# Attention outputs stored unnormalized with their row sums, and divided where the experts gather them

## Chip, cores and metric

One Trainium2 chip, one of its cores. The metric is the device time of one execution in microseconds (us). The engines are named as in the profile: PE (matmul) and PEld (its weight loads), DVE (vector), ACT (scalar), POOL (GpSimd) and SP, which only issues DMAs.

## The reference

Thresholded attention over 8 batches and 8 heads with 576 positions of 64 numbers each, followed by a mixture of 8 experts to which a hash of the token's id assigns each of the 4608 tokens.

```python
def _attn_ref(q, k, v, tau) -> np.ndarray:
    scale = 1.0 / np.sqrt(q.shape[-1])
    scores = scale * np.matmul(q, k.transpose(0, 1, 3, 2))
    thresh = np.max(scores, axis=-1, keepdims=True) - tau
    scores = np.where(scores >= thresh, scores, -1000000000.0)
    scores = scores - np.max(scores, axis=-1, keepdims=True)
    attn = np.exp(scores)
    attn = attn / (np.sum(attn, axis=-1, keepdims=True) + 1e-09)
    return np.matmul(attn, v).astype(np.float32)
...
    x = np.ascontiguousarray(attn_out.transpose(0, 2, 1, 3)).reshape(B * S, H * D)
...
    expert_idx = token_ids * np.int64(2654435761) % np.int64(E)
    for e in range(E):
        mask = expert_idx == e
        xe = x[mask]
        h = np.maximum(xe @ w1[e], 0.0)
        out[mask] = h @ w2[e]
```

x has 4608 rows of 512 numbers; w1 is 8 x 512 x 1024, w2 is 8 x 1024 x 512. All is float32.

## The kernel before

**Order.** The kernel is written with the Tile layer, inside blocks of `manual_schedule`: within such a block each engine runs its instructions in the order in which they stand in the program. The attention with all that runs beside it is one block, and the last steps of expert 0's first layer and the loop over the experts are others. An engine starts an instruction when its semaphores allow, and nothing behind it on that engine starts sooner.

**Attention.** Two heads of one batch make a pair p; there are 32 pairs, NP, in the order hp (which two heads, 0 to 3), then batch. A pair has five steps s; step n of the whole loop is 5p + s. Step 0 holds the last 64 rows of both heads, steps 1 to 4 hold 128 rows of each. A step's work is spread over three steps of the loop:

- `score` (L222, PE): scores into one of two PSUM buffers `sc`.
- `negate` (L233, DVE): copies -score into `ns` with the row's minimum, which frees `sc`; POOL makes the threshold `thr` (L240).
- `expo` (L247, ACT): exp into `w`.
- `mask` (L258, DVE), one step later: drops what is under the threshold, and gives the row sums `rs`.
- `turn_w` (L269, PE), two steps later: turns w through the single PSUM buffer `tr`; `put_wT` (L285 and L290, ACT) copies it to SBUF.
- `av_part` (L300, PE): the product with v into the PSUM tile `av`, a pair later, at steps 1 to 4; `put_oT` (L316, ACT) copies its halves.
- `turn_o` (L269, PE), two pairs later at step 0: turns them back into `av`, rows on partitions.
- `add_eps` (L330, POOL), L686 (DVE, reciprocal) and `put_xm` (L339, DVE): row sums plus 1e-9, their reciprocals, and the multiplication out of `av` into `xm`. Three DMAs on SP (L345, L350) then write xm to the DRAM tensor `x_scratch` of 4608 x 512, in pieces of 128 numbers.

The next `av_part` overwrites `av`, so it has to wait until `av` has been read.

**Routing** is done beside the attention, by small DVE instructions (`route`) and by POOL's DMAs (`scatters`).

**Expert 0 early.** From pair 26 on, POOL gathers for expert 0's five blocks kt of 128 rows the pieces hp = 0, 1, 2 (`fetch_early`, `fetch_0`, L113): 15 gathers, three for each block, at the steps 3, 4 and 0. At the last step (n = 160, LAST, and after) `early_xT` turns them, and `early_h` multiplies them with w1: 48 parts, called through `fill`, eight blocks of 128 columns, each into one of the two `sc` buffers, which a DVE copy (L594) frees. After the last pair's output come, in program order, the DVE copies of the indices (L753 to L761), the rest of `route` (to L488), the five gathers of the pieces hp = 3, `fill` for 30 parts, and `early_xT` for the last pieces (L563, L577). `late_h` adds the missing quarter.

**Experts.** For each expert two layers run, as products of seven blocks (`seven`, L859) with sums beforehand and afterwards on DVE (L791, L794) and copies on ACT; four PSUM buffers `bank2` rotate. `fetch(e)` gathers five blocks of whole rows of x into `xg`, `turn_x` turns them: five DVE transposes (L956) into `xq`, and 16 DMAs on SP (`move`, L964) into `xT`. Both are called from `side1` and `side2`, which run between the products of the two layers. `put_out` writes the results. A last loop takes rows beyond an expert's capacity, as many blocks as the routing counts.

## Time and profile before

| | us |
|---|---|
| median of 3 runs (949.88 to 950.99) | 950.64 |
| the profiled execution | 951.87 |
| its span, first to last instruction | 950.2 |
| PE busy in the span | 935.2 (98%) |
| DVE busy | 733.9 (77%) |
| ACT busy | 478.6 (50%) |
| POOL busy | 306.2 (32%) |
| L258, DVE, 288 instructions | 225.9 |
| L247, ACT, 288 instructions | 220.3 |
| L233, DVE, 288 instructions | 205.3 |

The attention takes about the first 455 us, expert 0's early part lies on its end, and from about 500 us on the experts run. The page has the span in 40 slices of 23.75 us, each digit a busy share in tenths. A row of a group gives the line, the engine, the operation, out<-in by the program's names with shapes, the count, and then busy time and mean time of one. A row in order of time begins with its start and its length in us; in brackets stands the idle time before it and what ended it. One engine's rows can overlap, since its instructions are pipelined. A matmul's end is modelled, its start is not.

### The profile page before, as it was taken

Reading aid. Unit: us, or ns where it says so; the run is one execution under the profiler, and the core shown is the slowest. Engines: PE = TensorE matmul, PEld = TensorE weight load, DVE = VectorE, ACT = ScalarE, POOL = GpSimd, SP = SyncE. Lnnn points to the kernel's source line nnn. Section 1 sums busy time; section 2 is a strip of 40 time slices with the busy share of each in tenths; the row PEclk is TensorE's granted clock in tenths of the full one; section 3 lists DMA queues with packets and bytes.
Section 4 is the critical chain, followed back from the end, with each engine's and each line's share of the span. In section 5 each row is a group of like instructions: output and inputs, shape, how many; then the busy total and the mean of one; then the engine's idle time right before and its main releaser. Section 6 shows DMA issues by size and latency. Waiting matters only on the chain. (4 is left out here: it accounts for less than half of the span.)

```text
span 950.2 us, 21041 instructions
## 1 busy us (share of the span) xinstructions
PE 935.2 (98%) x7779; PEld 645.2 (68%) x7779; DVE 733.9 (77%) x1638; ACT 478.6 (50%) x778; POOL 306.2 (32%) x413
## 2 busy tenths in 40 slices
PE   7999999999999999999999999999999999999996
PEld 4666666666666666666667777777777777777784
DVE  7999999999999999999456756756667566575541
ACT  6988888888898898888320211202112031120310
POOL 4233233237766733565043300403013030110202
PEclk9999999999999999999999999999999999999999
DMA  7355456445438857841017444344443445311101
GB/s 177 87 142 131 107 134 148 100 124 137 105 90 212 210 158 156 196 103 35 26 37 216 156 93 174 96 147 160 115 151 91 143 157 142 128 55 32 50 1 51
DMA packets 113510, 113.31 MB, mean 119 GB/s; under 512 B 31182, under 2 KB 88014, under 8 KB 113408
## 3 DMA queue, kind: packets, MB, share of 16 engines
q1 hardware_dynamic: 105168, 92.84, 36.9%
q0 software_dynamic: 7808, 18.91, 6.7%
q8 instruction: 63, 1.03, 0.5%
q14 instruction: 39, 0.32, 0.1%
q10 hardware_dynamic: 432, 0.21, 0.1%
HBM read 81.99 MB, written 21.72 MB: 109 GB/s over the span
## 5 line engine op out<-in xcount | busy, mean ns | idle before, releaser
L247 ACT ACTIVATE w<-ns,nmx 128x576 f32<-128x576 f32 x288 | 220.3, 776 | 32.8 <-DVE ns L233 32.5
L258 DVE SCALAR_TENSOR_TENSOR w<-ns,thr,w 128x576 f32<-128x576 f32 x288 | 225.9, 816 | 0.7 <-POOL thr L240 0.6
L233 DVE TENSOR_SCALAR_CACHE_REDUCE ns<-sc 128x576 f32<-128x576 f32 x288 | 205.3, 744 | 4.4 <-PE sc L222 3.5
L222 PE MATMUL sc<-k_sb,q 64*128 64x288 f32 (+1 forms) x1280 | 178.7, 423 | 1.1 <-DVE drop L650 0.6
L269 PEld LDWEIGHTS tr<-ident,w 64*128 64x128 f32 x2624 | 106.6, 139 | 88.4 <-ACT wT_b L290 26.4
L240 POOL TENSOR_SCALAR thr<-nmx,drop 128x2 f32<-128x2 f32 (+1 forms) x160 | 103.4, 646 | 184.0 <-DVE ns L233 173.3
L938 POOL DMA_INDIRECT out_dram<-o_sb,gidx x39 | 47.7, 1222 | 292.3 <-ACT o_sb L934 278.9
L269 PE MATMUL tr<-ident,w 64*128 64x64 f32 x2624 | 139.0, 230 | 2.6 <-ACT wT_a L290 2.0
L869 ACT COPY p<-bank 128x600 f32<-128x600 f32 (+1 forms) x22 | 14.4, 654 | 201.4 <-PE bank L859 200.6
L222 PEld LDWEIGHTS sc<-k_sb,q 64*128 64x128 f32 (+1 forms) x1280 | 92.5, 178 | 23.1 <-DVE ns L233 9.9
L300 PE MATMUL av<-wT_a,v 128*64 128x320 f32 (+1 forms) x704 | 100.7, 419 | 0.0
L859 PE MATMUL bank<-h,w_sb 128*128 128x300 f32 (+1 forms) x384 | 97.3, 410 | 0.9 <-DVE h L609 0.9
L866 ACT ACTIVATE h<-h 128x600 f32<-128x600 f32 x56 | 39.4, 703 | 114.6 <-DVE h L794 114.1
L290 ACT COPY wT_a<-tr 128x512 f32<-128x512 f32 (+1 forms) x128 | 81.7, 638 | 19.8 <-PE tr L269 19.5
L859 PE MATMUL bank<-xT,w_sb 128*128 128x300 f32 x336 | 89.4, 416 | 0.0
L859 PEld LDWEIGHTS bank<-h,w_sb 128*128 128x128 f32 x384 | 72.9, 190 | 22.9 <-DVE h L609 1.3
L290 ACT COPY wT_b<-tr 128x512 f32<-128x512 f32 (+1 forms) x128 | 81.2, 635 | 6.6 <-PE tr L269 4.3
L300 PE MATMUL av<-wT_b,v 128*64 128x256 f32 x640 | 83.2, 389 | 0.0
L859 PEld LDWEIGHTS bank<-xT,w_sb 128*128 128x128 f32 x336 | 63.9, 190 | 21.0
L859 PE MATMUL bank<-h_s,w_s 128*128 128x300 f32 (+1 forms) x256 | 64.3, 410 | 0.0
L300 PEld LDWEIGHTS av<-wT_a,v 128*64 128x64 f32 x704 | 43.9, 137 | 28.8 <-issue 0.3
L859 PE MATMUL bank<-x_s,w_s 128*128 128x300 f32 x224 | 61.5, 423 | 0.0
(147 smaller groups left out, 1110.3 us busy)
## 6 DMA issues: line engine op xcount, KB each, us to landing
w_sb<-in_moe_w_dram SPq DMA_DIRECT2D x16, 2048.0 KB
q<-in_q_dram SPq DMA_DIRECT2D x62, 288.0 KB
v<-in_v_dram SPq DMA_DIRECT2D x32, 256.0 KB
x_scratch<-xm SPq DMA_DIRECT2D x32, 256.0 KB
xT<-xq SPq DMA_DIRECT2D x84, 80.0 KB
k_sb<-in_k_dram SPq DMA_DIRECT2D x31, 144.0 KB
k_sb<-in_k_dram SPq DMA_DIRECT2D x32, 112.0 KB
x_scratch<-xg SPq DMA_DIRECT2D x9, 256.0 KB
```

What stands on the lines that cost most here:

```text
L222: nc.tensor.matmul(sc[out_rows, i, 0:S2], lhsT=q_sb[rows, h, q0:q1], rhs=k_sb[rows, h], start=True, stop=True)
L233: nc.vector.tensor_scalar(out=ns[:].rearrange("p (i s) -> p i s", i=2), in0=sc[:, :, 0:S2], scalar1=-1.0, scalar2=None, op0=ALU.mult, op1= ...
L240: nc.gpsimd.tensor_scalar(out=thr[:, 0:j + 1], in0=stats[n][0][:, 0:j + 1], scalar1=drop[:], scalar2=None, op0=ALU.add)
L247: nc.scalar.activation(w, nss[n, j][:], AF.Exp, bias=stats[n][0][:, j:j + 1], scale=-1.0)
L258: nc.vector.scalar_tensor_tensor(out=w, in0=nss.pop((n, j))[:], scalar=stats[n][1][:, j:j + 1], in1=w, op0=ALU.is_le, op1=ALU.mult, accum_ ...
L269: nc.tensor.transpose(dst[:, r, 64 * c:64 * c + 64], src[rows, c0:c0 + P], ident[rows, rows])
L290: nc.scalar.copy(dst, tr[:, :, 0:64 * n_c].rearrange("p r (c q) -> p r c q", c=n_c))
L300: nc.tensor.matmul(av[64 * j:64 * j + 64, g, c0:c1], lhsT=v_sb[:, c, 64 * j:64 * j + 64], rhs=wT[g][:, i, c0:c1], start=(c == 0), stop=stop)
L859: nc.tensor.matmul(ps[:, i, 0:width], lhsT=x[:, c, c0:c0 + P], rhs=y[:, c], start=c == 0, stop=c == n_k - 1)
L866: nc.scalar.activation(c, c, AF.Relu)
L869: nc.scalar.copy(p1, product(a11, b11))
L938: inst = nc.gpsimd.indirect_dma_start(out=out[:, :], out_offset=bass.IndirectOffsetOnAxis(ap=idx, axis=0), in_=o_sb, in_offset=None, bound ...
```

## The change

- `x_scratch` gets rows of 4 x 144 numbers instead of 4 x 128. A piece of 144 holds 8 numbers, 128 of data, and 8 numbers; the two heads' row sums stand in its columns 7 and 136. `xg` grows in the same way.
- `add_eps` writes the row sums plus 1e-9 into `xm` itself (two tiles that are kept, by turns). The reciprocal at step 2 is gone.
- `put_xm` is an ACT copy of `av` into `xm`, without a factor. At step 0 it stands ahead of `expo`; before, the DVE instruction stood behind `negate` and `expo`.
- A new `divide` on DVE takes the reciprocals of the sums in gathered rows and multiplies the rows by them. It is called for the early pieces of expert 0 at step 2 of pairs 27 to 31, for its last pieces behind their gathers, ahead of the transposes for each block of the other experts, and in the last loop.
- Turning x for expert e + 2 begins at the end of expert e's second layer (two blocks), and ends in the first half of the next expert's first layer; before, it lay in both halves of that first layer.

```diff
-    x_dram = nc.dram_tensor("x_scratch", (N, DIN), FP32, kind="Internal").ap()
+    XP = P + 16
+    XW = HP * XP
+    x_dram = nc.dram_tensor("x_scratch", (N, XW), FP32, kind="Internal").ap()
...
-        gather(x_rows, xg_bufs[kt][:, P * hp:P * hp + P], gidx_0[:, kt, hp:hp + 1])
+        gather(x_rows, xg_bufs[kt][:, XP * hp:XP * hp + XP], gidx_0[:, kt, hp:hp + 1])
+
+    def pieces_of(x, hp0, hp1):
+
+        return x[:, XP * hp0:XP * hp1].rearrange("p (h m) -> p h m", h=hp1 - hp0)
+
+    def x_sums(x, hp0=0, hp1=HP):
+        return pieces_of(x, hp0, hp1)[:, :, 7:2 * D + 9:2 * D + 1]
+
+    def x_data(x, hp0=0, hp1=HP):
+        return pieces_of(x, hp0, hp1)[:, :, 8:2 * D + 8]
+
+    def divide(x, hp0=0, hp1=HP):
+        rec = consts_r.tile([P, HP, 2], FP32, name="rec")[:, 0:hp1 - hp0]
+        nc.vector.reciprocal(rec, x_sums(x, hp0, hp1))
+        data = x_data(x, hp0, hp1).rearrange("p h (j d) -> p h j d", j=2)
+        nc.vector.tensor_tensor(out=data, in0=data,
+                                in1=rec[:, :, :, None].to_broadcast([P, hp1 - hp0, 2, D]),
+                                op=ALU.mult)
...
+            xm = xm_bufs[p % 2]
             rs = rss.pop(p)
-            for i, cols in ((0, 9), (9, 1)):
-                nc.gpsimd.tensor_scalar(out=rec[:, i:i + cols], in0=rs[:, i - i // 9:i - i // 9 + cols],
-                                        scalar1=1e-9, scalar2=None, op0=ALU.add)
-            recs[p] = rec
+            cols = slice(7, 2 * D + 9, 2 * D + 1)
+            for dst, src in ((xm[:, 0:NQ, cols], rs[:, 0:8].rearrange("p (t j) -> p t j", j=2)),
+                             (xm[:, NQ, cols], rs[:, 8:9].to_broadcast([P, 2]))):
+                nc.gpsimd.tensor_scalar(out=dst, in0=src, scalar1=1e-9, scalar2=None, op0=ALU.add)
...
-            nc.vector.tensor_tensor(
-                out=xm[:].rearrange("p t (j d) -> p t j d", j=2),
-                in0=av[:, :, 0:NS * D].rearrange("p j (t d) -> p t j d", t=NS),
-                in1=rec[:].rearrange("p (t j) -> p t j", j=2)[:, :, :, None]
-                .to_broadcast([P, NS, 2, D]), op=ALU.mult)
+            xm = xm_bufs[p % 2]
+            nc.scalar.copy(xm[:, :, 8:2 * D + 8].rearrange("p t (j d) -> p t j d", j=2),
+                           av[:, :, 0:NS * D].rearrange("p j (t d) -> p t j d", t=NS))
...
+        nc.vector.memset(x_sums(xg_bufs[0]), 1.0)
+        for xm in xm_bufs:
+            nc.vector.memset(xm[:, :, 0:8], 0.0)
+            nc.vector.memset(xm[:, :, 2 * D + 8:XP], 0.0)
...
-                if s == 2 and 0 <= q < NP:
-                    nc.vector.reciprocal(recs[q][:], recs[q][:])
+                if s == 2 and 0 <= n - G0 - 7 < NS * KT:
+                    divide(xg_bufs[(n - G0 - 7) // NS], 0, HP - 1)
...
                     negate(n, 0)
+                    if s == 0 and p >= 2:
+                        put_xm(p - 2)
                     expo(n, 0)
                 if s == 0 and p > 0 and not placed:
                     next(pieces)
-                if s == 0 and p >= 2 and n != LAST:
+                if n == LAST + NS:
                     put_xm(p - 2)
...
             for kt in range(KT):
                 fetch_0(kt, HP - 1)
+            for kt in range(KT):
+                divide(xg_bufs[kt], HP - 1, HP)
             fill(FO * 2 * (CO - 1) - 18)
...
-                return lambda: nc.vector.transpose(
-                    out=xq[:, :, 32 * k:32 * k + 32],
-                    in_=xg_bufs[k][:].rearrange("p (d a) -> p d a", a=32))
+                def both():
+                    divide(xg_bufs[k])
+                    nc.vector.transpose(
+                        out=xq[:, :, 32 * k:32 * k + 32].rearrange("p (h b) a -> p h b a", h=HP),
+                        in_=x_data(xg_bufs[k]).rearrange("p h (b a) -> p h b a", a=32))
+                return both
...
-                turns = turn_x(e + 1) if more else []
+                turns = pend if e else turn_x(1)
+                pend = []
...
-                        if step > 2:
-                            run(turns, 1 if g == 0 else 2)
+                        if g == 0 and step > 2:
+                            run(turns, 1 if step < 5 else 6)
...
                         if e + 2 < E:
                             fetch(e + 2)
+                            pend.extend(turn_x(e + 2))
                     else:
                         run(x_work, 2)
+                    if step == 5:
+                        run(pend, 2)
...
             gather(x_dram, xg_bufs[0][:], idx[:, 0:1])
+            divide(xg_bufs[0])
```

More of the change, by code (lines that the diff above doesn't have):

```diff
@@ L79 @@
     w_pool = ctx.enter_context(tc.tile_pool(name="w_pool", bufs=2))
+    consts_r = ctx.enter_context(tc.tile_pool(name="consts_r", bufs=2))
     sc_stack = ctx.enter_context(ExitStack())
@@ L104 @@
     ov_i = consts.tile([P, NOV + 1], I32, name="ov_i")
-    xg_bufs = [consts.tile([P, DIN], FP32, name=f"xg_{i}") for i in range(KT)]
+    xg_bufs = [consts.tile([P, XW], FP32, name=f"xg_{i}") for i in range(KT)]
     xT_0 = consts.tile([P, CO, CAP], FP32, name="xT_0")
@@ L135 @@
          tc.tile_pool(name="a_o", bufs=1) as a_o, \
-         tc.tile_pool(name="a_x", bufs=2) as a_x, \
+         tc.tile_pool(name="a_x", bufs=1) as a_x, \
          tc.tile_pool(name="rt_sb", bufs=1) as rt_sb, \
@@ L158 @@
         av = ps_av.tile([P, 2, 512], FP32, name="av")
-        kts, rss, recs, scs, nss, stats, ws = {}, {}, {}, {}, {}, {}, {}
+        xm_bufs = [a_x.tile([P, NS, XP], FP32, name=f"xm_{i}") for i in range(2)]
+        kts, rss, scs, nss, stats, ws = {}, {}, {}, {}, {}, {}
         def load_pair(p):
@@ L322, in x_place @@
             hp, b = divmod(p, B)
-            return b * S, hp * P
+            return b * S, hp * XP
         def add_eps(p):
-            rec = a_st.tile([P, 2 * NS], FP32, name="rec")
+            xm = xm_bufs[p % 2]
             rs = rss.pop(p)
-            for i, cols in ((0, 9), (9, 1)):
-                nc.gpsimd.tensor_scalar(out=rec[:, i:i + cols], in0=rs[:, i - i // 9:i - i // 9 + cols],
-                                        scalar1=1e-9, scalar2=None, op0=ALU.add)
-            recs[p] = rec
+            cols = slice(7, 2 * D + 9, 2 * D + 1)
+            for dst, src in ((xm[:, 0:NQ, cols], rs[:, 0:8].rearrange("p (t j) -> p t j", j=2)),
+                             (xm[:, NQ, cols], rs[:, 8:9].to_broadcast([P, 2]))):
+                nc.gpsimd.tensor_scalar(out=dst, in0=src, scalar1=1e-9, scalar2=None, op0=ALU.add)
         def put_xm(p):
-            rec = recs.pop(p)
-            xm = a_x.tile([P, NS, P], FP32, name="xm")
-            nc.vector.tensor_tensor(
-                out=xm[:].rearrange("p t (j d) -> p t j d", j=2),
-                in0=av[:, :, 0:NS * D].rearrange("p j (t d) -> p t j d", t=NS),
-                in1=rec[:].rearrange("p (t j) -> p t j", j=2)[:, :, :, None]
-                .to_broadcast([P, NS, 2, D]), op=ALU.mult)
+            xm = xm_bufs[p % 2]
+            nc.scalar.copy(xm[:, :, 8:2 * D + 8].rearrange("p t (j d) -> p t j d", j=2),
+                           av[:, :, 0:NS * D].rearrange("p j (t d) -> p t j d", t=NS))
             r0, c0 = x_place(p)
             nc.sync.dma_start(
-                out=x_dram[r0:r0 + TAIL, c0:c0 + P].rearrange("(t p) m -> p t m", p=P),
+                out=x_dram[r0:r0 + TAIL, c0:c0 + XP].rearrange("(t p) m -> p t m", p=P),
                 in_=xm[:, 0:NQ])
             for j in range(2):
-                cols = slice(D * j, D * j + D)
-                nc.sync.dma_start(out=x_dram[r0 + TAIL:r0 + S, c0 + D * j:c0 + D * j + D],
-                                  in_=xm[64 * j:64 * j + 64, NQ, cols])
+                cols = slice(XP // 2 * j, XP // 2 * j + XP // 2)
+                nc.sync.dma_start(
+                    out=x_dram[r0 + TAIL:r0 + S, c0 + XP // 2 * j:c0 + XP // 2 * j + XP // 2],
+                    in_=xm[64 * j:64 * j + 64, NQ, cols])
         def route():
@@ L563, in early_xT @@
                     nc.tensor.transpose(tr[:, r // 64, 64 * i:64 * i + r1 - r],
-                                        xg_bufs[kt][r:r1, P * co:P * co + P],
+                                        xg_bufs[kt][r:r1, XP * co + 8:XP * co + 8 + P],
                                         ident[r:r1, r:r1])
@@ L677 @@
                     nc.sync.dma_start(
-                        out=x_dram[r0:r0 + DIN, DIN - P:].rearrange("(t p) m -> p t m", p=P),
-                        in_=xg_bufs[0][:].rearrange("p (t m) -> p t m", m=P))
+                        out=x_dram[r0:r0 + DIN, XW - XP:].rearrange("(t p) m -> p t m", p=P),
+                        in_=xg_bufs[0][:].rearrange("p (t m) -> p t m", m=XP))
                 q = p - 1
@@ L1054 @@
             gather(x_dram, xg_bufs[0][:], idx[:, 0:1])
+            divide(xg_bufs[0])
             tr = bank2()
             for co in range(CO):
-                nc.tensor.transpose(tr[:, 0, co * P:co * P + P], xg_bufs[0][:, co * P:co * P + P],
-                                    ident[:])
+                nc.tensor.transpose(tr[:, 0, co * P:co * P + P],
+                                    xg_bufs[0][:, co * XP + 8:co * XP + 8 + P], ident[:])
             nc.vector.tensor_copy(xT_0[:, :, 0:P], tr[:, 0].rearrange("p (c q) -> p c q", c=CO))
```

## The prediction

> **What bounds the kernel now.** I read the page's slices first, then the windows, one per pair of heads, then the rows in order of time.

> ```profile
> PE   7999999999999999999999999999999999999996
> DVE  7999999999999999999456756756667566575541
> ```

> Up to slice 19 (about 452 us) two engines look full; afterwards only PE does. Of the two, one sets the pace and the other keeps up. The windows of two pairs (columns: length; busy PE, PEld, DVE, ACT, POOL with counts; clock, DMA share, GB/s):

> ```profile
> 298.89:312.78 13.89, 13.89 (x179) 8.81 (x176) 13.83 (x39) 12.29 (x21) 9.85 (x13) 1.00 0.49 110
> 312.78:326.67 13.89, 13.89 (x178) 8.81 (x175) 13.83 (x39) 12.28 (x21) 9.65 (x12) 1.00 0.97 257
> ```

> DVE is within 0.06 us of full, which invites the reading that 0.85 us taken off it shortens each pair. A matmul's end is modelled, so PE's busy time proves nothing; I compare starts. The PE rows below hold the same product of twelve and of eight matmuls twice: in the pair above, and in the last pair, where there are no scores left, ACT has little to do, and DVE sits idle for 7.15 and 5.10 us before its next row.

> ```profile
> 307.46 1.51 PE L300 MATMUL av<-wT_b,v 128*64 128x256 f32 x12
> 308.90 0.52 PE L269 MATMUL tr<-ident,w 64*128 64x64 f32 x10
> ...
> 310.66 1.08 PE L300 MATMUL av<-wT_b,v 128*64 128x256 f32 x8
> 311.68 0.52 PE L269 MATMUL tr<-ident,w 64*128 64x64 f32 x10
> ...
> 464.53 1.52 PE L300 MATMUL av<-wT_b,v 128*64 128x256 f32 x12
> 465.98 1.28 PE L587 MATMUL sc<-xT,w_sb 128*128 128x300 f32 x4
> 467.19 1.08 PE L300 MATMUL av<-wT_b,v 128*64 128x256 f32 x8
> 468.20 1.28 PE L587 MATMUL sc<-xT,w_sb 128*128 128x300 f32 x4
> ```

> From its first start to the next group's, twelve take 1.44 us in the full pair and 1.45 us in the idle stage; eight take 1.02 and 1.01 us. So these steps are PE's own. Start to start over a whole pair I find 12.04 us of columns and 1.74 us in some 25 changes of shape of 0.04 to 0.11 us each, the same at every place of one kind: 13.78 of 13.89. DVE's own steps (nine of 0.68 us at L233, nine of 0.74 us at L258, 0.73 and 0.12 us for L339 and L686) come to 13.6 us. **PE sets the pace of the attention; DVE is second by 0.3 us.** From 520 to 910 us I find no PE start later than 0.11 us behind its columns, with DVE near 63% busy: PE bounds the experts too.

> **The change, part by part.**

> 1. **DVE loses L339 and L686**: 0.73 + 0.12 = 0.85 us a pair. PE is the bound, so a regular pair gains nothing. What can be won is what irregular pairs have over 13.89: the starts of the turning of av give 13.93 to 14.43 us while DVE also runs the routing (2.1 us over in all up to the thirteenth pair) and one of 14.88 at 396 us, where POOL was late; 3.5 us in all. I take -2.6 (ends -3.5 and 0).

> 2. **ACT gets a copy of 128x640 out of PSUM.** Its nearest row has that very shape: L290, 692 ns. It stands behind the copy of tr and ahead of exp at the pair's first step:

> ```profile
> 299.71 0.82 DVE L339 TENSOR_TENSOR xm<-av,rec 128x640 f32<-128x640 f32 x1
> 299.77 0.58 ACT L290 COPY wT_b<-tr 128x512 f32<-128x512 f32 x1
> 300.25 0.78 ACT L247 ACTIVATE w<-ns,nmx 128x576 f32<-128x576 f32 x1
> ```

> ACT has 13.89 - 12.29 = 1.6 us free in a pair, 0.91 of it right behind this place (its exp at 302.71 waits for DVE). But the product at 300.93 overwrites av, and waits for whoever reads it: DVE was through at 300.52, ACT will start at 300.25, end at 300.94 and release at about 300.99. That is 0.06 to 0.12 us of PE in each of 30 pairs: +2.1 (ends 0 and 3.6). Exp runs 0.6 us later; its mask (L258) comes a step later, so nothing waits.

> 3. **Sums travel.** POOL's two additions stay (0.25 and 0.22 us), writing into xm. The three writes of a pair on SP stay three, with 288 KB for 256 and tails of 288 B for 256; gathers stay 20 and 35. SP is idle there; nothing on PE's path. The five extra memsets (some 0.1 us each) lie in DVE's 1.56 us wait for tau before 4.80 us. All at 0; without that cover, 0.5.

> 4. **Divides of early pieces** (five, at step 2 of pairs 27 to 31, where the reciprocal stood). Price: 0.12 for a reciprocal and, for 128x384, between 0.45 (128x288, L437) and 0.78 us (128x600, L794): 0.65 together. Their wait costs more: each needs the third gather of its block, issued 3.8 us before this place.

> ```profile
> 383.72 1.00 POOL L113 DMA_INDIRECT xg<-x_scratch,gidx  x1 [0.30 <-issue]
> ...
> 387.58 0.20 DVE L686 RECIPROCAL rec<-rec 128x10 f32<-128x10 f32 x1
> ```

> Time to landing of the third gathers: 8.9 us at 383.7 (w2 of 2 MB is in flight, DMA share 1.08), 4.3 at 400.2, 5.2 at 412.8, 2.5 at 440.6, unseen at 426.7 (I take 3.9). DVE issues in order: behind the divide stand both L233 of the step, so PE's next scores (two sc buffers), ACT's exps, POOL's thr. Lateness is landing + 0.65 - 3.85; PE has about 1.05 us before it misses a buffer (L233 ends at 304.96, its scores start at 306.06). So 4.65, 0.2, 1.0, 0, 0: +5.9 (ends 2 and 9).

> 5. **Divides of the last pieces**, emitted behind the five gathers of the end and **ahead of** the fill whose copies (L594) free the two sc buffers. In the trace:

> ```profile
> 474.75 0.77 DVE L594 COPY h<-sc 128x600 f32<-128x600 f32 x1
> ...
> 480.91 1.00 POOL L113 DMA_INDIRECT xg<-x_scratch,gidx  x1 [0.30 <-issue]
> ...
> 469.86 16.43 PE L587 MATMUL sc<-xT,w_sb 128*128 128x300 f32 x64
> 486.22 0.69 PE L563 MATMUL tr<-ident,xg 64*128 64x64 f32 x10
> ```

> Blocks of twelve matmuls at 0.2525 us fill one buffer: the third block of this row (at 469.86 + 24 x 0.2525 = 475.9) needs the copy of 474.75. Now that copy stands behind five divides, the last of which waits for the gather of 480.91. These landed 2.6 to 4.2 us after issue: 484.0 with 3.1. A divide of 128x128 lies between the rows of 128x36 (0.18) and 128x288 (0.45): 0.4 with its reciprocal; the copy 0.78: PE resumes at 485.2, 9.3 us late. x is written 0.3 us sooner by an idle ACT, a release costs 0.1 to 0.2: +9.2 (ends 8; 11.5 with a landing of 4.2 and a sum of w2, 1.22, in front). All PE work of the row still follows, so nothing hides it.

> 6. **Clock.** After a stretch with little matmul work the granted clock fell:

> ```profile
> 14.00:18.00 4.00, 2.55 (x40) 1.38 (x40) 4.00 (x11) 3.44 (x6) 1.43 (x2) 1.00 0.81 186
> 18.00:22.00 4.00, 4.00 (x32) 2.51 (x30) 4.00 (x13) 2.79 (x5) 2.12 (x5) 0.57 1.08 189
> ```

> A mean of 0.57 over 4 us is 3.4 us at half speed, which costs up to 1.7 us. Two stalls (pair 27 and the fill) may each bring one: 1.5 each, +3.0 (ends 0 and 3.4). [...]

> 7. **Experts.** 35 divides of whole rows, 128x512, between 0.45 and 0.78 and so 0.68, plus 0.12: 0.8 each, 28 us of DVE in all, hidden by DVE's idle third; uncovered they would be 28. Turning x is also drawn forward, two blocks at the end of layer 2 and four in the first half of layer 1, so its DMAs start earlier. Only the first expert is tight: five divides put its turning 4 us later, x lands at about 527.0 for 523.2, x_s follows, and the next layer's product at 526.80 and a PSUM buffer some 5 us on come 0.2 and 0.5 us late: +0.7 (ends 0 and 4).

> **Sum**: -2.6 + 2.1 + 5.9 + 9.2 + 3.0 + 0.7 = +18.3. The profiled execution took 951.87 (span 950.2, 1.7 around it), so 970.2 by it; the median of the runs shown, 950.64, stands 1.2 below it: **969 us**.

> **Rivals.**

> *DVE was the bound* (ends on the other side): 31 pairs lose 0.85 us, -26.4, and parts 4 to 7 stay at 18.8: 943. For it: 13.83 of 13.89 us busy. Against: the PE steps above, and DVE rows that wait for scores. It decides once pairs fall under 13.89 - 18.8 / 31 = 13.28 us. 0.10.

> *A stall is hidden*: the copies L594 run ahead of the divides, or landings are quicker. Without 9.2 and its clock 958; without 5.9 and its clock 962. For it: the sums of w2 at 475.44, written later, do run between the copies. Against: no L594 row runs ahead of a DVE instruction written before it. 0.15.

> *ACT becomes the bound*: 12.29 + 0.69 of 13.89 leaves 0.9 us, and its copies of tr let PE go on. If 0.5 us a pair shows on PE: +15, 984. Against: the 0.91 us wait right behind. 0.05.

> *The gains alone*: neither stall nor ACT's copy shows, -2.6: 948; 0.02.

> **How the numbers follow.** The forecast has 0.68; its own range, parts not all at one end together, is 960 to 977. With the hidden stall below and some of ACT above, 8 in 10 lie in 955 to 979. Differences over 0.2% count as seen (the runs shown spread over 0.12%). Faster 0.11 (the first rival and part of the last), same 0.03, slower 0.86.

> **What would show it.** Regular pairs at 13.9 to 14.0 us with DVE near 13.0 busy; L339's place on ACT with about 0.69 us; a DVE gap before the first early divide near 386 us and a pair of some 18 us; PE idle for about 9 us from 476 on, L594 behind the last divide, and the last turning of xg (L563, 486.22) some 27 us after the last turning of av (469.41) for 16.8 now; granted clock at half for a few us after each. Pairs under 13.5 us, or a PE row from 470 us on without a hole, would make it wrong.

## The result, and the profile after

The changed kernel takes 980.81 us (median of 5 runs, 976.49 to 982.36) for 950.99 us before in the same comparison. The ratio, estimated from all the runs, is 1.0306, with a 95% interval of 1.0288 to 1.0323 (the quotient of the two medians is 1.0314). The forecast was slower, at 969 us with 955 to 979. The direction was right, the time lies 11.8 us above the forecast and just above the range. The profiled execution is the fastest of the five, 976.49 us with a span of 974.5; the account below is made from it, and the 4.3 us from it to the median come at the end of the section on the prediction.

The slices of the changed kernel (tenths of each engine's time, 24.4 us a slice; PEclk is the granted clock):

```profile
PE   8999999999999999899969999999999999999996
DVE  8998999999999998799336785857768576785541
PEclk9999999999999999899979999999999999999998
```

Before the change PE was full in every slice but the first and the last; now the slices from 390 and from 487 us are at 8 and 6 tenths, and the granted clock is under full in the same two and in the last. The windows of seven stretches (columns: length; busy PE, PEld, DVE, ACT, POOL with counts; clock, DMA share, GB/s) say where the time went:

```profile
284.21:298.12 13.91, 13.91 (x178) 8.95 (x175) 13.11 (x37) 12.77 (x22) 10.00 (x13) 1.00 0.91 261
298.12:312.04 13.92, 13.92 (x178) 8.97 (x175) 13.08 (x37) 12.78 (x22) 10.27 (x13) 1.00 0.48 113
381.63:402.11 20.48, 16.49 (x178) 10.27 (x174) 14.12 (x39) 12.85 (x22) 8.33 (x12) 0.83 0.57 134
402.11:417.91 15.80, 14.52 (x179) 8.96 (x176) 13.88 (x39) 12.73 (x22) 8.19 (x12) 1.00 0.47 110
417.91:433.44 15.53, 14.59 (x178) 8.99 (x175) 13.97 (x39) 12.85 (x22) 8.28 (x12) 1.00 0.45 110
460.90:480.03 19.13, 16.71 (x142) 9.98 (x143) 2.88 (x7) 7.06 (x15) 0.47 (x2) 1.00 0.07 18
480.03:508.56 28.53, 19.16 (x76) 13.63 (x75) 13.94 (x37) 0.69 (x1) 7.32 (x5) 0.82 0.10 25
```

The first two are regular pairs: DVE has 0.75 us less to do, and the pair takes 13.91 and 13.92 us for 13.89. The other five hold the losses. Cut at the same events in both traces (starts of the turnings of av, start of the last turning of xg):

| stretch | before | after | difference |
|---|---|---|---|
| start to the 26th turning of av | 382.31 | 381.63 | -0.68 |
| the next three pairs (27 to 29 in the prediction) | 42.95 | 51.81 | +8.86 |
| two pairs | 27.42 | 27.46 | +0.04 |
| last step, to the last turning of av | 16.73 | 19.13 | +2.40 |
| last turning of av to last turning of xg | 16.81 | 28.53 | +11.72 |
| the rest (experts) | 463.95 | 465.98 | +2.03 |
| span | 950.17 | 974.54 | +24.37 |

**The first early divide**, rows in order of time (start, length, engine, line; in brackets the idle time before it and what ended it):

```profile
383.04 1.10 POOL L116 DMA_INDIRECT xg<-x_scratch,gidx  x1 [0.30 <-issue]
...
391.47 0.19 DVE L136 RECIPROCAL rec<-xg 128x6 f32<-128x6 f32 x1 [4.89 <-DMA xg<-x_scratch,gidx]
391.69 0.56 DVE L138 TENSOR_TENSOR xg<-xg,rec 128x384 f32<-128x384 f32 x1
...
392.98 2.29 PE L244 MATMUL sc<-k_sb,q 64*128 64x288 f32 x8 [3.99 <-DVE ns L255]
```

DVE stands for 4.89 us at a gather that took 8.3 us, and PE then waits 3.99 us for the copy of its scores, which is queued behind the divide. These eight matmuls take 2.29 us, the same eight of the regular pair at 298.74 take 1.19: the clock had just been halved, for 6.83 us. The pair is 6.56 us over 13.92. The divides of the next two pairs wait as well (with this one 8.3 us in three waits), and these pairs are 1.88 and 1.61 us over.

**The last divides**, rows in order of time:

```profile
480.49 6.33 PE L610 MATMUL sc<-xT,w_sb 128*128 128x300 f32 x24
...
492.48 1.01 POOL L116 DMA_INDIRECT xg<-x_scratch,gidx  x1 [0.30 <-issue]
...
494.94 0.17 DVE L136 RECIPROCAL rec<-xg 128x2 f32<-128x2 f32 x1 [0.68 <-DMA xg<-x_scratch,gidx]
495.14 0.29 DVE L138 TENSOR_TENSOR xg<-xg,rec 128x128 f32<-128x128 f32 x1
495.35 1.47 DVE L617 COPY h<-sc 128x600 f32<-128x600 f32 x2
496.18 2.87 PE L610 MATMUL sc<-xT,w_sb 128*128 128x300 f32 x5 [9.37 <-DVE h L617]
```

PE does two blocks of twelve and then has no buffer for 9.37 us, until the copies L617 run behind the fifth divide, which waited for the fifth gather.

**The last step** lost 2.4 us at a place that the prediction did not price:

```profile
460.90 0.52 PE L291 MATMUL av<-ident,oT 64*128 64x64 f32 x10 [0.20 <-ACT oT L338]
...
462.06 1.61 ACT L600 COPY xT<-sc 128x384 f32<-128x384 f32 x4
...
464.01 0.74 ACT L360 COPY xm<-av 128x640 f32<-128x640 f32 x1
...
464.81 1.84 PE L322 MATMUL av<-wT_a,v 128*64 128x320 f32 x12 [2.39 <-ACT xm L360]
```

The new copy L360 reads av, and the next product overwrites av. In the kernel before, the same place had the multiplication on DVE, where nothing of early_xT stands ahead of it, and PE did not wait:

```profile
453.31 0.82 DVE L339 TENSOR_TENSOR xm<-av,rec 128x640 f32<-128x640 f32 x1
...
453.84 1.61 ACT L577 COPY xT<-sc 128x384 f32<-128x384 f32 x4
...
454.18 1.84 PE L300 MATMUL av<-wT_a,v 128*64 128x320 f32 x12
```

On ACT the copy stands behind four copies of early_xT and one of tr. The same copy delays the two small products of the routing, once, beside the fifth pair (first the row before the change, then after it):

```profile
89.27 0.18 PE L410 MATMUL av<-row,u 128*128 128x8 bf16 x1
...
89.67 0.17 PE L429 MATMUL av<-row,u 128*128 128x8 bf16 x1 [1.33 <-ACT xm L360]
```

**The experts** lose 2 us at one place, in the second expert's first layer:

```profile
556.65 0.69 DVE L138 TENSOR_TENSOR xg<-xg,rec 128x512 f32<-128x512 f32 x1
557.37 0.71 DVE L985 STREAM_TRANSPOSE xq<-xg 128x512 f32<-128x512 f32 x1
558.01 0.74 DVE L821 TENSOR_TENSOR h<-bank,p 128x600 f32<-128x600 f32 x1
...
558.81 2.29 PE L886 MATMUL bank<-x_s,w_s 128*128 128x300 f32 x8 [1.97 <-DVE h L821]
```

PE needs the PSUM buffer that L821 reads, and L821 is queued behind the divides and turns of two blocks that are not needed until an expert later.

### The profile page after: what moved, and what is told of

Its sections match the earlier page's. It is cut to its first block, busy times and chain, and to the rows that moved or that the text cites. A ratio compares the mean times of both kernels' runs of the same rounds, so it can differ in the third digit from the quotient of the medians.

```text
span 974.5 us, 21151 instructions
## 1 busy us (share of the span) xinstructions
PE 938.9 (96%) x7779; PEld 651.5 (67%) x7779; DVE 750.0 (77%) x1669; ACT 494.3 (51%) x810; POOL 317.2 (33%) x413
## 3 DMA queue, kind: packets, MB, share of 16 engines
q8 instruction: 63, 1.03, 0.4%
## 5 line engine op out<-in xcount | busy, mean ns | idle before, releaser
L269 ACT ACTIVATE w<-ns,nmx 128x576 f32<-128x576 f32 x288 | 221.2, 779 | 11.6 <-DVE ns L255 11.3
L255 DVE TENSOR_SCALAR_CACHE_REDUCE ns<-sc 128x576 f32<-128x576 f32 x288 | 207.4, 753 | 19.3 <-PE sc L244 17.1
L262 POOL TENSOR_SCALAR thr<-nmx,drop 128x2 f32<-128x2 f32 (+1 forms) x160 | 108.6, 679 | 207.8 <-DVE ns L255 197.7
L291 PEld LDWEIGHTS tr<-ident,w 64*128 64x128 f32 x2624 | 108.8, 138 | 84.9 <-ACT wT_a L312 23.6
L244 PEld LDWEIGHTS sc<-k_sb,q 64*128 64x128 f32 (+1 forms) x1280 | 94.8, 178 | 26.2 <-DVE ns L255 10.6
L893 ACT ACTIVATE h<-h 128x600 f32<-128x600 f32 x56 | 39.4, 703 | 118.9 <-DVE h L821 118.9
```

The source lines that it names most:

```text
L244: nc.tensor.matmul(sc[out_rows, i, 0:S2], lhsT=q_sb[rows, h, q0:q1], rhs=k_sb[rows, h], start=True, stop=True)
L255: nc.vector.tensor_scalar(out=ns[:].rearrange("p (i s) -> p i s", i=2), in0=sc[:, :, 0:S2], scalar1=-1.0, scalar2=None, op0=ALU.mult, op1= ...
L262: nc.gpsimd.tensor_scalar(out=thr[:, 0:j + 1], in0=stats[n][0][:, 0:j + 1], scalar1=drop[:], scalar2=None, op0=ALU.add)
L269: nc.scalar.activation(w, nss[n, j][:], AF.Exp, bias=stats[n][0][:, j:j + 1], scale=-1.0)
L291: nc.tensor.transpose(dst[:, r, 64 * c:64 * c + 64], src[rows, c0:c0 + P], ident[rows, rows])
L893: nc.scalar.activation(c, c, AF.Relu)
```

## The experiments

The nine kernels ran on different chips. On one of them (e1 to e4, g1, g2) the kernel before takes 957 us, on the others 951, so every result is a ratio to the kernel before on the same chip. On that chip the 14th to the 22nd pair take 14.2 to 14.7 us in all six traces, with and without divides; the other traces don't show this, and the kernel before has no trace there.

| kernel | edit | ratio | 95% interval |
|---|---|---|---|
| the changed kernel | | 1.0306 | 1.0288 to 1.0323 |
| e1_last_behind_fill | last divides behind the fill | 1.0213 | 1.0182 to 1.0244 |
| e2_early_later | early divides two steps later | 1.0187 | 1.0167 to 1.0207 |
| e3_both | both | 1.0082 | 1.0062 to 1.0102 |
| e4_no_divides | the changed kernel without divides | 1.0067 | 1.0038 to 1.0096 |
| f2_three_waits_moved | e3 and three more places | 0.9995 | 0.9984 to 1.0005 |
| f3_vector_load | e3 and 0.8 us more on DVE a pair | 1.0072 | 1.0047 to 1.0098 |
| f4_tensor_kept_busy | changed kernel, work behind the hole | 1.0424 | 1.0399 to 1.0449 |
| g1_hole_filled | changed kernel, work in the hole | 1.0286 | 1.0245 to 1.0327 |
| g2_order_no_divides | f2 without divides | 1.0005 | 0.9988 to 1.0022 |

### The two places of the divides: e1, e2, e3

e1:

```diff
-            for kt in range(KT):
-                divide(xg_bufs[kt], HP - 1, HP)
             fill(FO * 2 * (CO - 1) - 18)
+            for kt in range(KT):
+                divide(xg_bufs[kt], HP - 1, HP)
```

> Only the five divides of expert 0's last pieces are moved, from ahead of the fill's remaining 30 parts to behind them. Theory (order on DVE): the copies that free the two score buffers no longer stand behind divides that wait for gathers, so the hole of 9.5 us in PE's starts at the end of the attention and the half clock of 10.2 us behind it (4.2 us of them with PE at work) both go: 28.5 us from the last turning of av to the last turning of xg fall to 16.8, and the time from 980.8 to about 969. Rival (the time goes to ACT's copy, or to the larger pieces in DMA): the hole stays or another takes its place, and the time stays above 977.

e2:

```diff
-                if s == 2 and 0 <= n - G0 - 7 < NS * KT:
-                    divide(xg_bufs[(n - G0 - 7) // NS], 0, HP - 1)
+                if s == 4 and 0 <= n - G0 - 9 < NS * KT:
+                    divide(xg_bufs[(n - G0 - 9) // NS], 0, HP - 1)
```

> Only the divides of expert 0's early pieces are moved, two steps later (step 4 of pairs 27 to 31 for step 2). Theory: the third gathers landed 8.3, 5.3, 4.9, 2.7 and 2.6 us after issue, and two steps are some 5.5 us, so DVE finds all of them landed; pairs 27 to 29 fall from 20.5, 15.8 and 15.5 us to 13.9, and the time from 980.8 to about 971. Rival (the gathers themselves hold POOL, and POOL holds the thresholds): the three pairs stay above 15 us, and the time above 977.

e3 has both edits.

> Both moves together. Theory: the two costs lie at different places and add up, so about 960; what remains over the 951 of before is ACT's copy at the last step (2.4), the routing's small matmuls (1.5), expert 1's first layer (2.1) and the half clocks that go with none of them. Rival (one hides behind the other): no better than the better one of the two, about 969.

In percent of the time before, e1 lies 0.93 under the changed kernel, e2 1.19 and e3 2.24. The first two add up to 2.12, within the intervals the same as the third, so the two places cost independently. In the windows of e1, the last step and the way to the last turning of xg:

```profile
467.13:487.89 20.76, 18.34 (x142) 10.49 (x142) 2.88 (x7) 7.06 (x15) 0.47 (x2) 0.92 0.06 17
487.89:504.70 16.81, 16.81 (x75) 12.47 (x74) 13.61 (x37) 0.69 (x1) 5.61 (x5) 1.00 0.17 42
```

The second takes 16.81 us again, to the hundredth what it took before the change; the five divides still run there, beside the fill. In e2, the three pairs and the same way:

```profile
386.11:400.36 14.25, 14.13 (x178) 8.88 (x174) 13.80 (x39) 12.87 (x22) 6.34 (x10) 1.00 0.69 168
400.36:414.53 14.17, 14.10 (x178) 8.81 (x174) 13.38 (x39) 12.90 (x22) 8.80 (x13) 1.00 0.54 126
414.53:429.48 14.95, 14.49 (x179) 8.87 (x176) 14.35 (x41) 12.99 (x22) 8.31 (x12) 1.00 0.48 115
...
478.80:507.00 28.20, 18.83 (x74) 13.70 (x74) 13.96 (x37) 0.69 (x1) 7.30 (x5) 0.82 0.10 25
```

Pairs of 14.2 to 15.0 us stand where 20.5, 15.8 and 15.5 stood, and the hole at the end is unchanged. Each edit removes its own stall only. The divides themselves are all still done, so it was their place in DVE's queue that cost, not their time.

### What the divides cost at all: e4

```diff
     def divide(x, hp0=0, hp1=HP):
+        return
```

> All divides are left out, so the experts get rows that are not divided by their sums; ACT's copy, the larger pieces and the moved turning of x stay. DVE has 0.85 us less in each pair than before. Theory (PE sets the pace of the pairs): pairs stay at 13.9, none under 13.85, and the time is about 955: 951 less some 2.5 in irregular pairs, plus 0.9 for 30 pairs at 0.03, 1.5 at the routing, 2.4 at the last step and up to 2 at the experts. Rival (DVE was the bound): pairs near 13.1 us and a time under 935. Rival (divides are not what costs): above 970.

Measured 1.0067, within the intervals the same as e3 with its divides. It is a poor separator: two of its pairs, at 415 and 433 us, take 17.5 us. In each, PE waits 1.7 us for ACT's copy of tr, the granted clock is then at half for 3.41 us, which is up to 1.7 us more (the mean clock of the execution is 0.991), and no divide is there to cause the wait; what does is open. So e4 doesn't give the price of the gains alone; g2 was made for that.

### Three more places: f2

In the last step `put_xm` moves ahead of early_xT; the routing's products are issued half a pair earlier; and the first expert's second layer leaves the two early divides to the next layer.

```diff
                 if n == LAST:
+                    put_xm(p - 2)
                     for k in (0, 2):
...
                 if n == LAST:
-                    put_xm(p - 2)
                     av_part(q, 0, (0, 1, 2))
...
             nc.vector.tensor_copy(row[:], incl[:, :, NTC - 1])
             yield
-            yield
...
             nc.vector.tensor_copy(cnt[:], tr[:, 0:2 * E])
             yield
+            yield
...
-                    if step == 5:
+                    if step == 5 and e:
                         run(pend, 2)
```

> The computation is whole. It is e3_both with three more pieces of order changed: in the last step ScalarE's xm copy stands ahead of the early_xT copies, the two routing products (L429, L430) are issued half a pair earlier, away from the xm copy, and the first expert's layer 2 no longer runs two divides and turns ahead of the next sums. Theory: what is left of the loss after e3_both (ratio 1.0082) is these three waits on the in-order queues, 2.55 us at the last step, 1.5 us at the routing products and 2.54 us at the first product of the second expert, 6.6 us together; the ratio falls to 1.0015 (0.9995 to 1.0035), and in the trace the three gaps of TensorE are under 0.5 us each. Rival one, the waits return elsewhere (the early_xT copies now late for the early products, the divides now late for the next expert's turn): ratio 1.005 or more, with a new gap of over 1 us behind one of the three places. Rival two, the copy on ScalarE itself is what costs, in every pair: ratio 1.008 as before, with the pairs longer than 13.95 us where the loads and scatters leave them alone.

Measured 0.9995, at the lower end of what was expected: no slower and no faster than the kernel before. The windows of the first pair with an early divide before it, of the last step and of the way to the last turning of xg:

```profile
380.38:394.30 13.92, 13.92 (x178) 8.98 (x174) 13.78 (x39) 12.77 (x22) 5.93 (x9) 1.00 0.77 174
451.16:468.27 17.11, 16.70 (x142) 9.97 (x142) 3.12 (x9) 7.06 (x15) 0.74 (x3) 1.00 0.07 20
468.27:485.08 16.81, 16.81 (x75) 12.47 (x74) 13.62 (x37) 0.69 (x1) 5.62 (x5) 1.00 0.16 42
```

In the last step the copy L360 now runs ahead of the copies of early_xT:

```profile
452.32 0.68 ACT L360 COPY xm<-av 128x640 f32<-128x640 f32 x1
...
452.89 1.63 ACT L600 COPY xT<-sc 128x384 f32<-128x384 f32 x4
...
453.06 1.83 PE L322 MATMUL av<-wT_a,v 128*64 128x320 f32 x12 [0.38 <-ACT xm L360]
```

PE's wait there is 0.38 us for 2.39, and the two pairs around the routing's products take 28.33 us for 29.63. Between 370 us and the end PE's rows show no other wait over 0.35 us but the 0.87 us between expert 0's layers, which the kernel before has as well (0.87). The whole loss was made of waits at five places and the half clock behind some of them, and with the places mended nothing is left of it; nor of a gain.

### Was DVE's relief worth anything: f3, g2

f3 gives DVE in each pair about what the change took from it:

```diff
+                if s == 0 and p >= 2 and n < LAST:
+                    nc.vector.tensor_tensor(out=busy[:], in0=busy[:], in1=busy[:], op=ALU.mult)
```

> The computation is whole; one VectorE instruction is added to each pair of e3_both, a multiplication of a 128x640 tile of ones by itself, about 0.8 us (from 691 ns for the 128x512 multiplication), about what the change took from VectorE in each pair (0.85 us). Theory: TensorE sets the pair's 13.9 us both before and after, and the 0.85 us taken from VectorE bought nothing; given back, they cost at most 0.1 us a pair, 3 us over 28 pairs: ratio 1.008 to 1.012. Rival, VectorE set the pair before or shares in setting it: 0.3 to 0.8 us a pair come back, 8 to 22 us: ratio 1.017 to 1.031.

Measured 1.0072 for e3's 1.0082. The window of one pair:

```profile
299.10:313.01 13.91, 13.91 (x179) 8.88 (x175) 13.68 (x38) 12.76 (x22) 10.02 (x13) 1.00 0.49 112
```

The added instruction takes 0.82 us. DVE is busy for 13.68 us, in the changed kernel's pair 13.08, and the pair takes 13.91 us. By this run the rival "DVE was the bound" is out: none of the 8 to 22 us came.

> This is f2_three_waits_moved without any divide: the rows go to the experts undivided, the reciprocals and the multiplications are left out, and everything else stays. Theory: with the places mended the divides lie wholly beside TensorE's work and cost nothing, and taking 0.85 us a pair off VectorE wins nothing either, so the kernel stands where f2 stands, 0.9995 (0.998 to 1.0008). Rival one, the divides still cost 2 to 4 us in the pairs of 14.6 us at 394 to 423 us and in the experts: 0.9955 to 0.9975, with those pairs under 14.2 us. Rival two, as in e4_no_divides, pairs near 420 us of up to 17.5 us, for which no divide is the reason: 1.003 to 1.008.

g2 is f2 with e4's edit. Measured 1.0005, its interval overlapping that of f2. Leaving all divides out of a kernel in which they stand in harmless places wins nothing that can be measured. Its traced execution has one pair of 17.5 us like those of e4, on the same chip, so some 3.5 us of that execution are this and not the divides; the bound on what they cost is no finer than that. The two pairs of 14.6 us that f2 has from 394 us on stand here without divides too (14.7 and 14.6), so they are not the divides' either.

### The clock behind the hole: f4, g1

```diff
-            fill(FO * 2 * (CO - 1) - 18)
+            fill(25)
             tr = ps_tr.tile([P, 2, 512], FP32, name="tr")
+            for _ in range(80):
+                nc.tensor.transpose(tr[:, 0, 0:P], ident[:], ident[:])
+            fill(FO * 2 * (CO - 1) - 18 - 25)
```

> The computation is whole. It is the changed kernel with 80 transposes of the identity (0.107 us each at the full clock) issued in TensorE's 9.5 us hole behind the 31st turning, into a bank that is not in use there. Theory: the hole's price is its length plus the halved clock behind it; with TensorE kept at work the granted clock stays at 1.0 there, and the 4.24 us of work that ran at 0.5 takes 2.1 us less: ratio 1.0284 (1.027 to 1.0295) for 1.0306, the hole's length unchanged. Rival one, the clock costs nothing there, as VectorE's chain of divides and copies still ends last: ratio 1.0306, with the granted clock at 1.0. Rival two, the clock is halved whatever TensorE does: 0.5 for 10 us in the trace again, ratio 1.0306.

f4 missed its place: the hole comes after 10 of these 30 parts, not after 25, so the 80 transposes ran behind the hole, the mean clock of the execution is the changed kernel's 0.988, and the way from the last turning of av to the experts takes 9 us more than in the changed kernel (48.3 us for 39.4). It says nothing on the question. g1 has `fill(10)` and the rest behind.

> The computation is whole. It is the changed kernel with 80 transposes of the identity issued inside TensorE's 9.5 us hole, between the twelfth and the thirteenth early product behind the 31st turning (f4_tensor_kept_busy had them behind the hole). Theory: the granted clock stays at 1.0 there, the hole's length from the last early product to the next stays 9.5 to 9.8 us, and the 4.24 us of work that ran at half clock takes 2.1 us less: ratio 1.0284 (1.0265 to 1.03) for 1.0306. Rival one, VectorE's divides and copies still set the end, so the clock costs nothing: 1.0306 (1.030 or more) with the granted clock at 1.0. Rival two, the clock is halved whatever TensorE does: 0.5 for 10 us in the trace, 1.0306 or more.

The windows of the changed kernel, from the last turning of av to the hole, the hole, and on to the experts:

```profile
480.03:486.40 6.37, 6.37 (x35) 4.86 (x34) 5.59 (x21) 0.69 (x1) 1.14 (x2) 1.00 0.19 53
486.40:496.18 9.78, 0.41 (x2) 0.00 (x0) 6.15 (x15) 0.00 (x0) 6.18 (x4) 0.69 0.16 35
496.18:519.46 23.28, 23.28 (x89) 16.64 (x90) 6.01 (x8) 4.78 (x10) 2.78 (x6) 0.91 0.07 17
```

The same three in g1:

```profile
491.46:498.08 6.62, 6.62 (x35) 5.01 (x35) 5.84 (x21) 0.69 (x1) 1.39 (x2) 1.00 0.19 54
498.08:507.72 9.64, 8.90 (x82) 8.66 (x80) 5.91 (x15) 0.00 (x0) 5.94 (x4) 1.00 0.16 36
507.72:528.90 21.18, 21.18 (x89) 15.39 (x90) 5.99 (x8) 4.78 (x10) 2.76 (x6) 1.00 0.08 18
```

The same 89 matmuls behind the hole take 21.18 us for 23.28: 2.1 us for the clock, as expected, with the hole as long as it was. The ratio, 1.0286, agrees, but its interval holds 1.0306 too; and g1's traced execution (mean clock 0.988) has a pair of 17.6 us and half clock at the last step and in the second expert's first layer, none of which the changed kernel's has. So the windows decide, not the total.

## Why the prediction was right, and where it was wrong

The step that failed is step 2: it gave ACT's copy the place that it has in a regular pair, and no term for the last step (+2.4 us) and the routing (+1.3 us), where other work stands ahead of the copy or waits for it. Steps 4, 5 and 7 were too small besides, by 1.5, 1.0 and 1.3 us. Of the 11.8 us between forecast and median, 6.1 lie in the steps below. The median stands 4.3 us above the profiled execution, the forecast had taken off 1.2 us because the profiled execution before stood that much above its own median, and 0.2 us lie outside the span.

By its own steps, in the profiled execution (+24.4 us of span where the sum was +18.3):

| step | predicted | measured |
|---|---|---|
| 1, 2: regular and irregular pairs up to the last step | -0.5 | -0.64 |
| 2 at the last step | 0 | +2.40 |
| 4, with half of 6 | +7.4 | +8.86 |
| 5, with half of 6 | +10.7 | +11.72 |
| 7 | +0.7 | +2.03 |

**Right.** PE sets the pace of the pairs, and taking 0.85 us from DVE buys nothing in a regular one: 13.92 us for 13.89 with the 0.85 us taken away, and 13.91 us with 0.82 us given back in f3. The hole at the end was foretold at 9.3 us and is 9.4 of waiting, for the reason given: copies L617 behind divides that wait for gathers. The rival of a hidden stall had the sums of w2 for it, which do run between the divides (L818 at 487.74 and 490.09 in the changed kernel); the copies do not. The first early divide with its clock was put at 4.65 + 1.5 = 6.15 us and is 6.56 (the sign "a pair of some 18 us" left the clock out: the pair takes 20.48).

**Right by luck, the first row.** The start to the last step came out at -0.64 for -0.5, but 1.15 us of this were won ahead of the first turning of av (31.70 us for 32.85). That is scatter and no gain of the change: in the traces of the experiments, all with the change, this turning starts between 31.64 and 32.98 us. The pairs themselves cost 0.51 us where -0.5 was forecast. Of the first thirteen pairs, eleven lost the 1.6 us that they had over a regular pair, as step 1 said; but the first is now 0.2 us over it and the fifth 1.8, where it was 0.5.

**Wrong, step 2.** "It stands behind the copy of tr and ahead of exp at the pair's first step" is true of 30 pairs. The cost was worked out for these, 0.06 to 0.12 us each, and measured smaller (0.03); the copy's length, 0.70 us at 299.48, was right as well. At the last step the order is another: early_xT's four copies stand ahead, which the trace before and the code both showed. That is +2.40, with no term in the sum and no room in the range. The routing's products, which also touch av and wait for the same copy, wait 1.33 us; this is most of the fifth pair's excess, and lies within the first row of the table. f2 shows both: with the order changed, 2.0 and 1.3 us come back.

**Too small, step 4.** The pairs after the first were put at 0.2 and 1.0 us late and are 1.88 and 1.61 over the regular pair; and the 14.88 us pair whose excess step 1 counted as won is one of them. (The formula gives 0.05 us for the first of the two, not 0.2.) The landings taken, 4.3 and 5.2 us, are 5.3 and 4.9 in the new trace, and DVE stands for 1.89 and 1.52 us of them, so the divide's place comes 3.4 us after the gather's issue, where the formula has 3.85. With these numbers it gives 1.5 and 1.1 us. The remaining 0.4 and 0.5 us would lie in the grace of 1.05 us before PE misses a buffer; no run shows that apart.

**Too small, step 7.** The step looked at when x is turned and lands. The wait came from the other edit in it, the two blocks drawn forward: they stand in DVE's queue ahead of L821. f2, which leaves these two to the next layer, has no such wait.

**Right in size, step 6.** 2.1 us at the hole by g1, where 1.5 was put; this is 0.6 of the 1.0 us by which step 5's row is over. At the first early divide 5.0 us of PE's work lie in the halved stretch, which is up to 2.5 us and fits the 6.56 us (3.99 of waiting, 2.5 of clock).

**Left open.** The other four executions of the changed kernel took 3.0 to 5.9 us more than the profiled one; their mean clock was 0.986 for its 0.988. A part is the clock: 0.002 of 978 us is 4 us at half clock, at most 2 us of time. That the rest is longer waits for gathers is argued only: e1, which keeps the early divides in their place, spreads over 5.3 us, e2 and e3, which don't, over 1.5 and 1.8. The range had no term for it.

## What to carry to other kernels

An instruction that moves to another engine is to be followed through every place where it is issued, the first and the last step above all: what stands ahead of it there is other work than in the regular step. On an engine that runs in order, an instruction that waits for a DMA is to stand behind everything that the bound engine needs from it; here two moves by a few lines were worth 2.2% and three more another 0.9%. And relief for the second busiest engine was worth nothing here, because the first one's own steps set the pace.

## What the runs showed of the hardware

```profile
459.11:461.66 2.55, 0.23 (x8) 0.09 (x4) 1.04 (x4) 2.55 (x6) 0.46 (x2) 1.00 0.00 0
461.66:465.20 3.54, 3.48 (x13) 1.34 (x13) 0.00 (x0) 0.00 (x1) 0.00 (x0) 0.52 0.35 96
```

The clock is at 1.00 in the hole and at 0.52 in the 3.54 us behind it, and the last step takes 20.76 us for 19.13. A hole of 2.55 us, shorter than the halved stretch behind it, was enough here. The price, 1.6 us, is two thirds of the wait itself.

In the changed kernel the wait of 1.97 us ahead of the second expert's x_s products left the clock at 1.00. Cut along the clock's changes into stretches of 3.413 us, the traces of the two kernels have five stretches at full clock with half clock behind them, with 0.00, 0.04, 1.21, 1.24 and 1.96 us of PE busy; of the other whole ones none has less than 1.49. From 1.49 to 1.96 us both occur. PE's ends are modelled, so these figures are rough.

**The clock beside transposes.** In g1's hole of 9.64 us PE was busy for 8.90 us with 82 matmuls, 80 of them transposes of 128x128 in float32, products with the identity, and the granted clock was 1.00 there and in the 21.18 us behind it. In the changed kernel's hole of 9.78 us, with 0.41 us of PE busy, it was 0.69, and 0.91 in the 23.28 us behind it.
